# Attention with two head mixes and two MLPs on one core: the second mix on eight 64x32 tiles with VectorE transposes, and PSUM as four shared pairs of banks

## The chip, the cores and the metric

One core of a Trainium2 chip. The metric is device time in microseconds for one execution of the whole program (median of three runs); the profile is of one further execution of the same kernel. TensorE is PE in the rows (PEld its weight loads), VectorE DVE, ScalarE ACT, GpSimd POOL, SyncE SP.

## The reference

Four batches, 12 heads, 448 positions, 64 wide. The scores of all heads are mixed across heads before the softmax and the weights are mixed across heads after it; then two MLPs (768 to 2048 to 768) run over 1792 tokens.

```python
scores = scale * np.matmul(q, k.transpose(0, 1, 3, 2))
scores = np.einsum('bhij,hg->bgij', scores, w_pre)        # first mix
attn = exp(scores - max) / (sum + 1e-09)
attn = np.einsum('bhij,hg->bgij', attn, w_post)           # second mix
x = np.matmul(attn, v)                                    # tokens x 768
h = x @ moe_w_in;   x = (s * relu(h) ** 2 + b) @ moe_w_out
h = x @ moe2_w_in;  out = (h * cos(h)) @ moe2_w_out
```

## The kernel before

A planner (`Plan`) holds every step with a position, an engine (or a choice of ACT and DVE), a cost, what it comes after and which places of which ring it takes. `Plan.run` walks through time and gives each engine that is free the ready step with the lowest position; the instructions are then written in that order, so each engine's queue is fixed when the kernel is built. `STEP`, `OFF`, `W1`, `AVP` and the like are the numbers that set positions.

The attention works on blocks of 120 or 110 query rows. For each pair of heads, `heads` transposes k and q on TensorE (L306), four pieces of 112 x 128 each, and copies them out of PSUM. `scores` (L336) multiplies q by k for the two heads of a pair on the two 64-row halves of the array; each result (110 or 120 rows x 448) is copied to `s` and goes by DMA into `m`, where the 12 heads x 5 query rows (60) lie on the partitions, and two such groups make a tile of 10 query rows. There are 180 tiles, done in 90 pairs. For each pair of tiles:

- `mix` (L393): four matmuls, 60x64 weights `wp`, 448 columns, on four 64x64 tiles of the array, into two banks `p`.
- `rmax` (L403): a maximum of each bank on DVE, twice. `expo` (L409): the exponential of each bank on ACT, with a sum, twice.
- DVE adds 1e-9 (L412) and takes the reciprocal (L413); `weigh` (L417, POOL) multiplies the mix matrix by it into `w`.
- `mixt` (L427): the second mix. The exponentials `e` are the weights, 60 x 112 keys at a time, and `w` (60 columns) is what moves: 16 matmuls, on the two 64-row halves, which puts the keys on the partitions of the result `a` (112 x 480, one bank for each tile).
- `keep` (L235 on DVE or L233 on ACT): each bank is copied into `at`, which holds a half batch.

When a half batch is complete, `prod` (L464) multiplies it by v for four heads at a time: 16 matmuls of 230 or 220 columns over 112 keys, on two 64-column tiles, and `xo` is copied and stored to `x`. There are 24 such products. PSUM's eight banks are split: two for scores, transposes and products with v (ring `ps`), two for the second mix (`pa`), four for the first mix (`pp`).

The MLPs (L704, L767, L797) begin when their token columns of `x` are loaded, and their weights are prepared on ACT, DVE and POOL (L626 to L654). Every fp32 matmul of the attention stands in the trace as two LDWEIGHTS and two MATMUL records.

Of the kernel before, what the change touches and what calls it, by code (L numbers as in the profile page):

```python
# [10 lines left out]
F32 = mybir.dt.float32  # L11
# [5 lines left out]
ALU = mybir.AluOpType  # L17
# [5 lines left out]
CH = 112  # L23
TOKENS = (512, 512, 256, 512)
# [6 lines left out]
class Hold:  # L31


    def __init__(self, ring):
        self.ring, self.users, self.tile = ring, 0, None


class Plan:
# [5 lines left out]
    def __init__(self):  # L44
        self.steps, self.cap, self.turns = [], {}, {}
# [7 lines left out]
    def hold(self, ring):  # L53
        return Hold(ring)
# [14 lines left out]
    def run(self):  # L69
# [30 lines left out]
        def blocked_until(i, t):  # L100
# [3 lines left out]
            for h in st[i]["take"]:  # L104
                k = need.get(h.ring, 0)
# [11 lines left out]
        while n_done < len(st):  # L117
# [7 lines left out]
            while again:  # L125
                again = False
                for e in free:
# [34 lines left out]
                    for h in s["take"]:  # L162
                        taken[h.ring].append(h)
                    for h in s["use"]:
                        h.users -= 1
                        if not h.users:
                            freed_at[h] = end + s["lag"] + self.SYNC[e]
                            heapq.heappush(events, freed_at[h])
# [26 lines left out]
STEP = 2374.9  # L195
# [3 lines left out]
def attention(pl, tc, q, k, v, w_pre, w_post, cst, x, mid, left, right, psl, psr):  # L199
# [6 lines left out]
    NG = H // 2  # L206

# [42 lines left out]
    def idle(pos, n, cost, after):  # L250
        hz = pl.hold("ps")

        def run():
            hz.tile = ps_s.tile([128, 512], F32, tag="s", name="idle")
# [7 lines left out]
    mask = one.tile([128, 2, G], F32, name="mask")  # L262
    w12 = one.tile([128, 2, H], F32, name="w12")
    wp = one.tile([128, 64], F32, name="wp")
    wq = one.tile([128, H, G], F32, name="wq")
    d_id = dma(-5200, lambda: ident, lambda: cst[:, 0:128], 65536, cost=450.0)
    d_mk = dma(-500, lambda: mask.rearrange("p a g -> p (a g)"), lambda: cst[:, 128:128 + 2 * G], 5120)
    z0 = pl.add(-9e9, "dve", 100.0, lambda: (nc.vector.memset(w12, 0.0), nc.vector.memset(wp, 0.0)))
# [7 lines left out]
        out=wq, in0=w12[:, 1].rearrange("p (g o) -> p g o", o=1).to_broadcast([128, H, G]),  # L276
        in1=mask[:, 0].rearrange("p (o r) -> p o r", o=1).to_broadcast([128, H, G]), op=ALU.mult), d_w + [d_mk])
# [6 lines left out]
    at_all = at_p.tile([128, 2, 4, H, width[0]], F32, name="at")  # L284
# [3 lines left out]
    def heads(what, b, g, p):  # L288
        src = k if what == "k" else q
        ht = turned[what, b, g] = pl.hold(f"{what}{g}")  # L290
        hr, hp = scratch[what == "q"] if b == 0 else pl.hold("r"), pl.hold("ps")

        def raw(new=False):
            if b == 0:
                i = g * 8 * D
                return at_all[:CH, int(what == "q")].rearrange("p c h w -> p (c h w)")[:, i:i + 8 * D].rearrange("p (z h d) -> p z h d", h=2, z=4)
            if new:
                hr.tile = r_p.tile([CH, 4, 2, D], F32, tag="r", name="raw")
            return hr.tile
        d = dma(p - 6000, lambda: raw(True), lambda: src[b, 2 * g:2 * g + 2].rearrange("h (p z) d -> p z h d", z=4), CH * 8 * D * 4,  # L300
                [s_open] if b == 0 else [], take=[hr] if b else [], behind=m_done[0][-1:] if b else [], two=b == 0 and g < 2, rate=300.0)

        def trans():
            hp.tile = ps_s.tile([128, 512], F32, tag="s", name="t" + what)[:, :S].rearrange("p (z w) -> p z w", z=4)
            for z in range(4):
                nc.tensor.transpose(hp.tile[:, z], raw()[:, z].rearrange("p h d -> p (h d)"), ident[:CH, :CH])  # L306
        a = pl.add(p, "pe", 400.0, trans, [d, d_id], take=[hp, ht], use=[hr])

        def evac(e):
# [45 lines left out]
    for g in range(NG):  # L355
        for what in "kq":
            heads(what, 0, g, PRO[0] * g)
# [521 lines left out]
```

## Time and profile before

| | us |
|---|---|
| median of 3 runs (1410.46 to 1412.24) | 1411.2 |
| profiled execution, its own time | 1410.2 |
| its span in the trace | 1408.4 |
| PE busy | 1383.4 (98%) |
| DVE busy | 1095.8 (78%) |
| ACT busy | 665.8 (47%) |
| POOL busy | 429.7 (31%) |
| mean granted TensorE clock | 0.982 |

How to read it: the first second mix starts at 51 us and the last products with v end at 474 us; from about 498 us on PE runs MLP matmuls without a break. Matmuls overlap, and the ends of their records are modelled, so that the busy share of PE says little; the chain of waits, which gives each stretch of time to one cause, says more.

### The profile page before, as it was taken

The numbers are of one execution on the slowest core, as the hardware profiler recorded it, in microseconds if no ns is written. First come the engines' busy times: TensorE is split into PE (matmuls) and PEld (weight loads), VectorE is DVE, ScalarE is ACT, GpSimd is POOL, SyncE is SP. The second block draws the span as 40 slices with busy tenths as digits, with TensorE's granted clock in tenths as the row PEclk, the third lists the DMA queues.
The fourth block names the chain that finished last, engine by engine and source line by source line (L and its number), as shares of the span: only waits on it lengthen the run. The fifth ranks groups of instructions, "written<-read, shape, count | busy, mean of one in ns | idle before, by whom it ended". The sixth has DMA issues, their size and how long they took to land.

```text
span 1408.4 us, 25444 instructions
## 1 busy us (share of the span) xinstructions
PE 1383.4 (98%) x9753; PEld 1103.6 (78%) x9753; DVE 1095.8 (78%) x2052; ACT 665.8 (47%) x1385; POOL 429.7 (31%) x415
## 2 busy tenths in 40 slices
PE   7999999999999899999999999999999999999999
PEld 3466565666666688888888888889999999899998
DVE  3566666576577688889887787898799999998975
ACT  1575465465467454323232232466645545445442
POOL 2010000010012443423333243235554444554531
PEclk6899999999999999999999999999999999999999
DMA  6645456444444422221121212112121111211103
GB/s 132 183 129 146 143 138 156 138 130 140 139 148 141 142 68 68 68 67 58 54 71 34 67 47 65 36 34 68 46 68 46 57 57 45 69 45 57 56 35 123
DMA packets 120605, 123.80 MB, mean 88 GB/s; under 512 B 49476, under 2 KB 108324, under 8 KB 120484
## 3 DMA queue, kind: packets, MB, share of 16 engines
q1 hardware_dynamic: 117880, 120.43, 29.6%
q10 hardware_dynamic: 2604, 1.75, 0.5%
q8 instruction: 77, 1.26, 0.4%
q14 instruction: 44, 0.36, 0.1%
HBM read 72.43 MB, written 11.01 MB: 59 GB/s over the span
## 4 chain that ended last, share of the span: by engine, by line
PE 96%; DVE 1%; DMA 1%; ACT 1%; SPq 0%; issue 0%; POOL 0%; DVEq 0%; POOLq 0%
PE h L704 33%; PE o L797 17%; PE o L767 16%; PE a L427 11%; PE sps L336 7%; PE p L393 6%; PE vps L464 5%; PE tq L306 1%; PE tk L306 1%; DMA m<-s 0%; SPq L229 0%; DMA at<-in_q_dram 0%; DMA m<-x 0%; DVE s L235 0%; DVE x L680 0%
## 5 line engine op out<-in xcount | busy, mean ns | idle before, releaser
L652 POOL TENSOR_TENSOR cm<-ca,wh 128x384 f32<-128x384 f32 x128 | 160.8, 1258 | 363.3 <-ACT wh L646 362.6
L704 PE MATMUL h<-m,wh 128*128 128x512 f32 x672 | 217.0, 392 | 0.0
L704 PE MATMUL h<-x,wh 128*128 128x512 f32 (+1 forms) x768 | 192.0, 341 | 5.2 <-DVE x L680 3.8
L427 PEld LDWEIGHTS a<-w,e 60*112 60x112 f32 x2880 | 153.6, 176 | 50.8 <-issue 29.3
L654 POOL TENSOR_TENSOR wl<-cm,ce 128x384 fp32r<-128x384 f32 x128 | 147.5, 1154 | 93.4 <-DVE ce L650 87.3
L427 PE MATMUL a<-w,e 60*112 60x60 f32 x2880 | 161.6, 261 | 3.7 <-POOL w L417 3.5
L417 POOL TENSOR_TENSOR w<-wq,st 128x120 f32<-128x120 f32 x90 | 35.5, 396 | 396.5 <-DVE st L413 306.9
L704 PEld LDWEIGHTS h<-x,wh 128*128 128x128 f32 x768 | 133.0, 190 | 22.5 <-DVE x L680 4.8
L704 PE MATMUL h<-m,wl 128*128 128x512 f32 x384 | 150.6, 392 | 0.0
L704 PEld LDWEIGHTS h<-m,wh 128*128 128x128 f32 x672 | 125.4, 188 | 25.8 <-issue 0.7
L767 PE MATMUL o<-gl,wh 128*128 128x512 f32 (+1 forms) x384 | 139.6, 364 | 0.0
L767 PE MATMUL o<-gh,wl 128*128 128x512 f32 (+1 forms) x384 | 139.6, 364 | 0.0
L409 ACT ACTIVATE e<-p,st 128x448 f32<-128x448 f32 x180 | 113.2, 630 | 55.4 <-DVE st L403 41.6
L767 PE MATMUL o<-gh,wh 128*128 128x512 f32 (+1 forms) x384 | 139.3, 363 | 0.0
L704 PE MATMUL h<-x,wl 128*128 128x512 f32 (+1 forms) x384 | 130.9, 341 | 0.0
L403 DVE TENSOR_REDUCE st<-p 128x1 f32<-128x448 f32 x180 | 109.5, 618 | 21.7 <-PE p L393 19.4
L336 PE MATMUL sps<-kt,qt 64*110 64x448 f32 (+1 forms) x384 | 109.3, 613 | 6.7 <-DVE s L235 5.3
L797 PE MATMUL o<-wh,gl 128*128 128x384 f32 x448 | 114.3, 335 | 0.0
L797 PE MATMUL o<-wh,gh 128*128 128x384 f32 x448 | 114.2, 335 | 0.0
L797 PE MATMUL o<-wl,gh 128*128 128x384 f32 x448 | 114.2, 335 | 0.0
L744 POOL TENSOR_TENSOR tb<-ta,tb 128x512 f32<-128x512 f32 (+1 forms) x64 | 79.0, 1234 | 114.3 <-ACT tb L742 109.4
L806 DVE TENSOR_TENSOR acc<-acc,o 128x384 f32<-128x384 f32 x196 | 99.7, 545 | 14.3 <-PE o L797 14.2
(86 smaller groups left out, 2616.6 us busy)
## 6 DMA issues: line engine op xcount, KB each, us to landing
m<-s SPq DMA_DIRECT2D x144, 192.5 KB
raw<-in_moe_w_in_dram SPq DMA_DIRECT2D x64, 384.0 KB
raw<-in_moe_w_out_dram SPq DMA_DIRECT2D x64, 384.0 KB
m<-s SPq DMA_DIRECT2D x42, 210.0 KB
v<-in_v_dram SPq DMA_DIRECT2D x12, 448.0 KB
out_dram<-acc SPq DMA_DIRECT2D x13, 384.0 KB
raw<-in_k_dram SPq DMA_DIRECT2D x18, 224.0 KB
raw<-in_q_dram SPq DMA_DIRECT2D x18, 224.0 KB
```

The lines of the kernel that those rows point to most:

```text
L336: nc.tensor.matmul(out=hp[z].tile, lhsT=hq.tile[64 * z:64 * z + 64, i0:i0 + rows], rhs=hk.tile[64 * z:64 * z + 64], start=True, stop=True, ...
L393: nc.tensor.matmul(out=hp[y].tile[64 * z:64 * z + 64], lhsT=wp[64 * y:64 * y + (K if y else 64)], rhs=src[64 * y:64 * y + (K if y else 64) ...
L403: nc.vector.tensor_reduce(out=hst.tile[:, 0, y:y + 1], in_=hp[y].tile, axis=AX, op=ALU.max, negate=True)
L409: nc.scalar.activation(out=he.tile[:, y], in_=hp[y].tile, func=AF.Exp, bias=hst.tile[:, 0, y:y + 1], accum_out=hst.tile[:, 1, y:y + 1])
L427: nc.tensor.matmul(out=ha[z].tile.rearrange("p (c g r) -> p c g r", c=4, g=H)[:, c, :, y * G:(y + 1) * G], lhsT=he.tile[64 * z:64 * z + K, ...
L652: a = pl.add(p0 + 6 * dp, "pool", 1050, lambda hm=hm, ha=ha, flat=flat: nc.gpsimd.tensor_tensor(out=hm.tile, in0=ha.tile.bitcast(F32), in1 ...
L654: got.append(pl.add(p0 + 7 * dp, "pool", 1050, lambda hm=hm, he=he, flat=flat: nc.gpsimd.tensor_tensor(out=flat(1), in0=hm.tile, in1=he.ti ...
L704: nc.tensor.matmul(out=hp.tile, lhsT=w, rhs=cols(z_, j, k)[:, 0], start=(k == 0 and y == 0), stop=(k == KD - 1 and y == 2))
L744: a = pl.add(p + 7 * dp, "pool", n * 2.4 + 100, lambda h1=h1, h2=h2: nc.gpsimd.tensor_tensor(out=h2.tile, in0=h1.tile, in1=h2.tile, op=ALU ...
L767: nc.tensor.matmul(out=hp.tile, lhsT=w, rhs=x, start=(c == 0 and y == 0), stop=(c == 1 and y == 2))
L797: nc.tensor.matmul(out=hp[e].tile, lhsT=x, rhs=w[:, e * HD:(e + 1) * HD], start=(c == 0 and y == 0), stop=(c == 1 and y == 2))
L806: got.append(pl.add(p, "dve", 470, lambda e=e, hp=hp, view=view: nc.vector.tensor_tensor(out=view(), in0=view(), in1=hp[e].tile, op=ALU.ad ...
```

## The change

The second mix is turned round: `w` is now the weights, in pieces of 32 columns (6 heads x 5 rows and two columns of zeros), and `e` moves, 224 columns at a time. The 16 matmuls of a pair go to eight tiles of 64 rows x 32 columns. The result has the mixed rows on the partitions, so `keep` is now a VectorE transpose of 32x32 blocks, one for both banks of a pair (94 in all, 86 of them of two banks), and `at` has the keys on 64-partition halves, one half for each six heads. The product with v has 28 matmuls over 64 keys on four 64x64 tiles, in place of 16 over 112 keys on two; what moves there are pieces of 5 elements, 32 apart. v is loaded by two DMAs per four heads in place of one, in rows of 256 bytes.

PSUM is four tiles of two banks each (`bank`), and scores, transposes (now k and q together), both mixes and the products with v all take one such pair, whichever comes free first; at most two each for the first mix, the second mix, and the rest. One `tensor_reduce` takes the maximum of both banks. The addition of 1e-9 goes from DVE to POOL. k is now written with the same order of columns as q.

```diff
@@ Plan
+    def places(self, name, n):
+
+        self.slots[name] = [0.0] * n
...
+                if h.ring in self.slots:
+                    open_at = [a for z, a in enumerate(self.slots[h.ring]) if a is not None and (h.only is None or z in h.only)]
+                    if not open_at:
+                        return None
+                    when = max(when, min(open_at))
+                    continue
@@ attention
-    ps_s = pool(psl, "a_ps_s", N_PS, space=PSUM)
-    ps_a = pool(psl, "a_ps_a", N_PA, space=PSUM)
-    ps_p = pool(psr, "a_ps_p", N_PP, space=PSUM, side="right")
+    ps_l = pool(psl, "a_ps_l", space=PSUM)
+    ps_r = pool(psr, "a_ps_r", space=PSUM, side="right")
+    bank = [(ps_r if z > 1 else ps_l).tile([128, 2, 512], F32, name=f"ps{z}") for z in range(4)]
+    pl.places("u", 4)
...
-    at_all = at_p.tile([128, 2, 4, H, width[0]], F32, name="at")
+    NU = width[0] // G
+    at_all = at_p.tile([128, 2, KB, NU * 32], F32, name="at")
...
-        a = pl.add(p, "pe", 400.0, trans, [d, d_id], take=[hp, ht], use=[hr])
+        a = pl.add(p, "pe", 860.0, trans, [load["k"], load["q"], d_id], take=[hp, lim, ht["k"], ht["q"]], use=[hr["k"], hr["q"]])
...
-            copy(e, ht.tile.rearrange("p (w z) -> p z w", z=4) if what == "q" else ht.tile.rearrange("p (z w) -> p z w", z=4), hp.tile)
+                copy(e, ht[what].tile.rearrange("p (w z) -> p w z", z=4), bank[hp.slot][:, y, :S].rearrange("p (z w) -> p w z", z=4))
...
+        for z in range(2):
+            got.append(dma(p, lambda z=z: v_all[64 * z:64 * z + 64, c], lambda z=z: v[b, GH * z + 2 * c:GH * z + 2 * c + 2].rearrange("h (k p) d -> p (h k) d", p=64),
+                           64 * 2 * KB * D * 4, take=[] if z else [hv], behind=got[:1] + m_done[0][-1:], rate=200.0))
...
-        hp, hs = [pl.hold("ps"), pl.hold("ps")], pl.hold("s")
+        hp, lim, hs = pl.hold("u"), pl.hold("ps"), pl.hold("s")
...
-        hp, ha = [pl.hold("pp"), pl.hold("pp")], [pl.hold("pa"), pl.hold("pa")]
+        last = i >= NTL // 2 - 2
+        hp, ha = pl.hold("u", (2, 3) if last else None), pl.hold("u", (0, 1) if last else None)
+        limp, lima = pl.hold("pp"), pl.hold("pa")
...
-                nc.vector.tensor_reduce(out=hst.tile[:, 0, y:y + 1], in_=hp[y].tile, axis=AX, op=ALU.max, negate=True)
+            nc.vector.tensor_reduce(out=hst.tile[:, 0], in_=hp.tile, axis=AX, op=ALU.max, negate=True)
...
-        a = pl.add(p - OFF[3] * STEP, "dve", 75, lambda hst=hst: nc.vector.tensor_scalar(out=hst.tile[:, 2], in0=hst.tile[:, 1], scalar1=1e-9, scalar2=None, op0=ALU.add), got)
+        a = pl.add(p - OFF[3] * STEP, "pool", 200, lambda hst=hst: nc.gpsimd.tensor_tensor(out=hst.tile[:, 2], in0=hst.tile[:, 1], in1=eps, op=ALU.add), got)
...
-            for c in range(4):
-                for y in range(2):
-                    for z in range(2):
-                        nc.tensor.matmul(out=ha[z].tile.rearrange("p (c g r) -> p c g r", c=4, g=H)[:, c, :, y * G:(y + 1) * G], lhsT=he.tile[64 * z:64 * z + K, y, c * CH:(c + 1) * CH],
-                                         rhs=hw2.tile[64 * z:64 * z + K, y], start=True, stop=True, tile_position=(64 * z, 0))
+            for y in range(2):
+                for u in range(2):
+                    for c in range(2):
+                        for z in range(2):
+                            o = 64 * u + 32 * c
+                            nc.tensor.matmul(out=ha.tile[o:o + 32, z].rearrange("p (y k w) -> p y k w", y=2, w=32)[:, y], lhsT=hw2.tile[64 * z:64 * z + K, y, 32 * u:32 * u + 32],
+                                             rhs=he.tile[64 * z:64 * z + K, y].rearrange("p (k c w) -> p k c w", c=2, w=32)[:, :, c], start=True, stop=True, tile_position=(64 * z, o))
...
-                copy(e, at_all[:CH, slot].rearrange("p c h w -> p (c h) w")[:, :, col:col + R], h.tile.rearrange("p (c r) -> p c r", r=R))
+                nc.vector.transpose(out=at_all[:, slot].rearrange("p k (u w) -> p u k w", w=32)[:, unit:unit + 2 * m].rearrange("p (z y) k w -> p z y k w", y=2),
+                                    in_=h.tile[:, z:z + m].rearrange("p z (y k w) -> p z y k w", y=2, w=32))
...
+                for k in range(KB):
+                    for y in range(2):
+                        for z in range(2):
+                            w = (2 * pp + y) * G
+                            nc.tensor.matmul(out=bank[hp.slot][64 * y:64 * y + 64, z, :n].rearrange("p (u r) -> p u r", r=G), lhsT=v_all[64 * z:64 * z + 64, pp, y * KB + k],
+                                             rhs=at_all[64 * z:64 * z + 64, hf, k, :n // G * 32].rearrange("p (u w) -> p u w", w=32)[:, :, w:w + G],
+                                             start=(k == 0), stop=(k == KB - 1), tile_position=(64 * z, 64 * y))
...
-STEP = 2374.9
+STEP = 3468.7
...
-OFF = (2.256, 2.164, 1.349, -0.066)
+OFF = (2.847, 0.745, -0.81, 1.669)
```

The planner's costs and position numbers change too, so that the order of the steps is another one on every engine. The change names L393 as L426, L427 as L459, L464 as L498, L336 as L369, and its PSUM tiles ps_96 to ps_99 (one pair of banks each).

PE's queue where the products with v of the first batch's second half run, before (p is the first mix, a the second, sps the scores, vps a product with v):

```order
L336 MATMUL sps<-kt,qt 110x448 x2
L393 MATMUL p<-m,wp 64x448 x8
L427 MATMUL a<-w_1528,e 112x12x5 x16
L336 MATMUL sps<-kt,qt 110x448 x2
L427 MATMUL a<-w_1541,e 112x12x5 x16
L464 MATMUL vps<-at,v 64x220 x16
L427 MATMUL a<-w_1625,e 112x12x5 x16
L464 MATMUL vps<-at,v 64x220 x16
L393 MATMUL p<-m,wp 64x448 x4
```

The same stretch in the change:

```order
L426 MATMUL ps_98<-m,wp 64x448 x4
L459 MATMUL ps_96<-e,w_1306 32x224 x16
L369 MATMUL ps_99<-kt,qt 110x448 x2
L426 MATMUL ps_97<-m,wp 64x448 x4
L369 MATMUL ps_96<-kt,qt 110x448 x2
L459 MATMUL ps_99<-e,w_1348 32x224 x16
L369 MATMUL ps_98<-kt,qt 110x448 x2
L426 MATMUL ps_96<-m,wp 64x448 x4
L498 MATMUL ps_99<-at,v 64x220 x28
L459 MATMUL ps_97<-e,w_1380 32x224 x16
```

A second mix still has 16 matmuls, now 32 rows x 224 columns each; a product with v has 28 in place of 16; and all kinds of step take turns on the same four pairs ps_96 to ps_99.

VectorE's queue in the attention, before (st is a maximum, a sum or its reciprocal, at the kept second mix):

```order
L235 COPY at<-a 112x48x10
L235 COPY s<-sps 110x448
L403 TENSOR_REDUCE st<-p 128x1
L235 COPY at<-a 112x48x10
L403 TENSOR_REDUCE st<-p 128x1
L235 COPY s<-sps 110x448
L403 TENSOR_REDUCE st<-p 128x1
L412 TENSOR_SCALAR st<-st 128x2
L413 RECIPROCAL st<-st 128x2
```

And in the change:

```order
L473 STREAM_TRANSPOSE at<-ps_96 128x4x7x32
L433 TENSOR_REDUCE st<-ps_97 128x2
L433 TENSOR_REDUCE st<-ps_98 128x2
L473 STREAM_TRANSPOSE at<-ps_99 128x4x7x32
L258 COPY s<-ps_96 110x448
L444 RECIPROCAL st<-st 128x2
L258 COPY s<-ps_96 110x448
L433 TENSOR_REDUCE st<-ps_97 128x2
L444 RECIPROCAL st<-st 128x2
```

Each maximum and each transpose covers two banks, half of the kept second mixes no longer go to ACT, and the additions are gone from this queue. In VectorE's whole queue of the change stand 90 maxima, 94 transposes, 90 reciprocals, 80 copies of scores (102 before), 21 of k and q (24 before) and 48 of xo of half the length (34 whole ones before).

## Rows read from the trace of the kernel before

**Rows 1.** Busy time by stretch: stretch, its length, PE, PEld, DVE, ACT, POOL (counts), granted clock, DMA share, GB/s
```profile
0.00:50.00 50.00, 39.69 (x122) 15.15 (x123) 16.92 (x30) 10.19 (x20) 9.26 (x5) 0.62 0.70 157
50.00:440.00 390.00, 386.68 (x4565) 247.01 (x4563) 259.23 (x578) 228.03 (x547) 35.48 (x88) 1.00 0.50 143
440.00:500.00 60.00, 52.06 (x399) 40.66 (x400) 41.84 (x82) 30.64 (x67) 23.24 (x19) 0.89 0.39 123
500.00:1408.00 908.00, 905.02 (x4673) 800.76 (x4671) 777.84 (x1364) 396.97 (x755) 361.75 (x304) 1.00 0.19 58
```

**Rows 2.** The chain of waits from 50 to 440 us, shares by engine and line
```profile
by line: PE a L427 36.7%; PE p L393 20.0%; PE sps L336 19.1%; PE vps L464 17.3%; PE tq L306 2.1%; PE tk L306 1.8%; DVE qt L235 0.5%; DVE at L235 0.5%; DVE st L403 0.5%; issue 0.4%; ACT xo L233 0.3%; ACT qt L233 0.3%; POOL w L417 0.2%; ACT e
```

**Rows 3.** The same chain, pieces in order of time: start us, us, what
```profile
200.53 0.80 PE sps L336 x4
201.33 0.91 PE p L393 x8
202.24 1.71 PE a L427 x32
203.96 3.26 PE vps L464 x32
207.21 0.53 PE tk L306 x4
207.75 1.72 PE a L427 x32
```

**Rows 4.** Second mix by groups, 50 to 440 us: count | busy us, mean ns | idle before
```profile
L427 PE MATMUL a<-w,e 60*112 60x60 f32 x2720 | 151.2, 259 | 0.9 <-POOL w L417 0.7
L427 PEld LDWEIGHTS a<-w,e 60*112 60x112 f32 x2720 | 143.9, 175 | 45.6 <-issue 27.9 <-POOL w L417 15.3 <-POOL cm L652 0.7
```

**Rows 5.** VectorE by groups, 50 to 440 us
```profile
L403 DVE TENSOR_REDUCE st<-p 128x1 f32<-128x448 f32 x171 | 104.1, 618 | 17.4 <-PE p L393 15.2 <-POOL w L417 0.6
L235 DVE COPY s<-sps 110x448 f32<-110x448 f32 (+1 forms) x93 | 57.4, 622 | 8.2 <-PE sps L336 4.9 <-ACT e L409 0.2
L235 DVE COPY at<-a 112x480 f32<-112x480 f32 x86 | 56.4, 658 | 58.8 <-PE a L427 58.5
L235 DVE COPY xo<-vps 128x220 f32<-128x220 f32 (+1 forms) x32 | 17.8, 556 | 26.9 <-PE vps L464 26.3
L412 DVE TENSOR_SCALAR st<-st 128x2 f32<-128x2 f32 x85 | 14.1, 166 | 12.4 <-ACT e L409 12.2
L413 DVE RECIPROCAL st<-st 128x2 f32<-128x2 f32 x85 | 13.8, 162 | 2.0
```

**Rows 6.** ScalarE by groups, 50 to 440 us
```profile
L409 ACT ACTIVATE e<-p,st 128x448 f32<-128x448 f32 x172 | 108.2, 630 | 52.8 <-DVE st L403 39.0 <-DVE st L412 11.8 <-DVE st L413 1.6
L233 ACT ACTIVATE at<-a 112x480 f32<-112x480 f32 x84 | 48.5, 579 | 66.9 <-PE a L427 66.7
L233 ACT ACTIVATE qt<-tq 128x448 f32<-128x448 f32 x16 | 15.7, 982 | 20.2 <-PE tq L306 20.2
L233 ACT ACTIVATE kt<-tk 128x448 f32<-128x448 f32 x6 | 3.3, 543 | 2.1 <-PE tk L306 2.1
```

**Rows 7.** Busy time in a stretch of the MLPs, columns as in rows 1
```profile
560.00:700.00 140.00, 140.00 (x706) 118.82 (x705) 123.54 (x207) 43.51 (x82) 48.86 (x42) 1.00 0.21 62
```

**Rows 8.** Who waited for whom, 50 to 440 us: us in total, times, longest
```profile
POOL w L417 <- DVE st L413: 298.1, 61, 40.2
```

**Rows 9.** PE in order of time, start of the program: start us, us, what [idle before]
```profile
28.74 1.85 PE L336 MATMUL sps<-kt,qt 64*120 64x448 f32 x4 [0.77 <-DVE s L235]
31.34 1.85 PE L336 MATMUL sps<-kt,qt 64*120 64x448 f32 x4 [0.75 <-DVE s L235]
44.24 3.27 PE L393 MATMUL p<-m,wp 64*64 64x448 f32 x16
```

**Rows 10.** PE in order of time, end of the attention
```profile
451.44 3.24 PE L427 MATMUL a<-w,e 60*112 60x60 f32 x32 [2.21 <-POOL w L417]
487.24 0.51 PE L704 MATMUL h<-x,wh 128*128 128x512 f32 x1 [2.75 <-DVE x L680]
```

More of the change, by code (lines that the diff above doesn't have):

```diff
@@ L44, in __init__ @@
     def __init__(self):
[L45 removed]
+        self.steps, self.cap, self.turns, self.slots = [], {}, {}, {}
     def ring(self, name, cap, strict=True):
@@ L162, in run @@
                     for h in s["take"]:
-                        taken[h.ring].append(h)
+                        if h.ring in self.slots:
+                            w = self.slots[h.ring]
+                            h.slot = min((a, z) for z, a in enumerate(w) if a is not None and (h.only is None or z in h.only))[1]
+                            w[h.slot] = None
+                        else:
+                            taken[h.ring].append(h)
                     for h in s["use"]:
@@ L352, in scores @@
             m_done[n].append(dma(p + 1300, lambda z=z: place(z), lambda z=z: hs.tile[:rows, z], rows * S * 4, ev[z:z + 1], take=[hm] if g == 0 and z == 0 else [], use=[hs],
-                                 behind=m_done[n][:1], cost=870.0, two=n == 0))
+                                 behind=m_done[n][:1], cost=770.0, two=n == 0))
     for g in range(NG):
-        for what in "kq":
-            heads(what, 0, g, PRO[0] * g)
+        heads(0, g, PRO[0] * g)
         scores(0, g, PRO[0] * g + PRO[1])
@@ L429, in attention @@
-        a = pl.add(p, "pe", MIXT, mixt, [aw], take=ha, use=[he, hw2])
-        for z, t in enumerate(pair):
-            n, b_ = t["n"], t["b"]
-            half = (b_, (n % 4) // 2)
+            ha.tile = bank[ha.slot][:, :, :2 * KB * 32]
+            for y in range(2):
[5 more added lines that the diff above has]
+                                             rhs=he.tile[64 * z:64 * z + K, y].rearrange("p (k c w) -> p k c w", c=2, w=32)[:, :, c], start=True, stop=True, tile_position=(64 * z, o))
@@ L433, in attention @@
+        a = pl.add(p, "pe", MIXT, mixt, [aw], take=[ha, lima], use=[he, hw2])
+        halves = [t["n"] // 2 for t in pair]
+        for z in (0, 1) if halves[0] != halves[1] else (0,):
+            n, m = pair[z]["n"], 1 if halves[0] != halves[1] else 2
+            half = (n // 4, (n % 4) // 2)
             new = half not in hat
@@ new lines, in attention, with evac @@
+            a = pl.add(p + apart * 2 * pp, "pe", 2880.0, prod, kept[b, hf] + v_done[b, pp], take=[hp, lim], use=[hb, vh[b, pp]])
+            got = []
+            for z in range(2):
+                def evac(e, z=z, hp=hp, ho=ho, blocks=blocks, base=base, wid=wid):
+                    if z == 0:
+                        ho.tile = xo_p.tile([128, 2 * width[0]], F32, tag="xo", name="xo")[:, :2 * wid].rearrange("p (g n) -> p g n", g=2)
+                    c0 = 0
+                    for i0, rows in blocks:
+                        copy(e, ho.tile[:, z, i0 - base:i0 - base + rows].rearrange("p (r t) -> p r t", r=R), bank[hp.slot][:, z, c0:c0 + rows].rearrange("p (t r) -> p r t", r=R))
+                        c0 += rows
+                got.append(pl.add(p + apart * (2 * pp + 1) + 500, EV, (420.0, 420.0), evac, [a], take=[] if z else [ho], use=[hp, lim], behind=got[:1]))
+                if not late:
+                    free_psr.append(got[-1])
```

187 lines of the change are left out of this document (91 added, 96 removed).

## The prediction

> **What bounds the kernel now.** I read the busy time by stretch first, then the chain of waits, then the groups of each engine. The stretches divide the program [rows 1]: a start of 50 us at a granted clock of 0.62, the attention from 50 to 440 us at full clock, a passage of 60 us in which PE is idle for 8 us, and 908 us of MLPs in which PE is idle for 3. The change touches nothing in the last of these, so its effect must come out of the first three, above all out of 390 us of attention. There PE is idle for only 3.3 us [rows 1], but a busy PE is not PE at its peak; what matters is what each step takes on the chain. The chain of that stretch is 97% PE [rows 2]: second mix 36.7%, first mix 20.0%, scores 19.1%, products with v 17.3%, transposes 3.9%. VectorE is busy for 259 of the 390 us (66%) and ScalarE for 228 (58%) [rows 1]. So PE sets the pace here, and a shorter step on PE is worth its length as long as the other engines follow.
>
> **What a step on PE costs.** A first mix is 8 records of 448 columns on four tiles, so 2 rounds or 896 columns if the four work at once: 0.91 us [rows 3]. A product with v is 32 records of 230 columns on two tiles, 16 rounds or 3,680 columns: 3.26 us [rows 3]. The difference is 2.35 us for 2,784 columns, 0.844 ns a column, and what is left of a step is 0.154 us. Two and four tiles thus go with the same price, which says that tiles do work at once. By the same price a second mix, 32 records of 60 columns on two tiles, would take 16 x 60 x 0.844 ns + 0.154 = 0.96 us. It takes 36.7% of 390 us over 85 mixes (2,720 records of 32 each [rows 4]) = 1.68 us [rows 2]. Something other than columns that move holds it: (1.68 - 0.154) / 32 = 47.8 ns for each pair of a weight load and a matmul. Each load brings 112 columns of weights; in first mix and products it brings 64 and hides. 112 columns in 47.8 ns is 2.3 a ns, which at the granted full clock (2.4 GHz) is about one a cycle. I read it as the loads being in the way, one after the other.
>
> **The change, part by part.**
>
> *Second mix.* 32 records again, but of 32 columns of weights and 224 that move, on eight tiles: 4 rounds or 896 columns, 0.91 us, if all eight work at once and the loads (32 columns, about 14 ns at the rate above) hide. No row shows eight tiles or a load of 32 columns. From below: 0.91. From above: 48 ns for each pair whatever its width, or four tiles at once (8 rounds, 1.67 us), which both leave the 1.68 as it is; two at once would be worse and is a rival below. I take 0.91, since two and four tiles follow the price by columns: 90 x (1.68 - 0.91) = **-69.3 us**. The Trainium skill (TensorE: Matmul & The Clock Gate, "Wait — 56ns, not 53.3ns?") says that two matmuls never start closer than about 25 ns, however small. By it a mix would be 32 x 25 ns + 0.154 = 0.95 us, and the gain 4 us smaller; no row here has matmuls that close.
>
> *Product with v.* 56 records on four tiles: 14 rounds in place of 16. 14 x 230 x 0.844 ns + 0.154 = 2.87 us against 3.26, and 2.75 against 3.12 for 220 columns: 24 x 0.38 = **-9 us**. What moves are pieces of 5, which no row shows on PE; if that doubled the price of a column, it would cost 24 x 2.7 = +65 us. I take no charge and keep it as a rival.
>
> *Transposes of k and q together.* 24 steps in place of 48: 24 x 0.154 is 3.7, and half of it is hidden behind a neighbour of the same kind already: **-2 us** (0 to -4). Copies of k and q lie between the two that rows 6 shows, 0.54 and 0.98 us; either way it is a few us off the path.
>
> *VectorE.* One maximum over two banks: a row of 480 elements against one of 448 [rows 5] gives (658 - 622) / 32 = 1.1 ns an element, so 0.618 + 448 x 1.1 ns = 1.11 us against 2 x 0.618. The transpose of two banks has no row; by elements it is the same 1.11, against 0.658 for one bank on VectorE and 0.579 for the other on ScalarE [rows 5, 6]. In the stretch: maxima 94, transposes 94, reciprocals 14, scores 57.4 x 80/102 = 45, k and q some 14, xo 16, additions 0: 277 us in place of 259. ScalarE loses 48 us of copies [rows 6]. PE's own path shrinks to 390 - 85 x 0.77 - 21 x 0.38 - 2 = 314 us. VectorE would have to be busy for 88% of that. It is at 88% in a stretch of the MLPs where PE never waits [rows 7], so it can be; but in the attention each step crosses three engines several times, and now all kinds of step draw on the same four pairs of banks. A first mix holds a pair for about 0.9 + 1.1 + 2 x 0.83 us and the gaps between, over 4 us; a second mix over 2, scores about 2, a product with v about 4. Per pair of tiles that is some 10 us of pairs against 4 x 3.5 that there are, 70%. So PE will wait at times where it waits hardly at all now. Bounds: nothing (88%, rows 7), or VectorE at its present 66%, which would need 420 us and undo the gain. I take 83%, nearer to rows 7, where PE is also the one that sets the pace: 334 us, **+20 us** of new waits on PE.
>
> *Addition on POOL.* One more hop between the sums and the weights of the second mix. POOL is busy for 35 of 390 us [rows 1] and spends 298 us waiting for the reciprocal [rows 8]; nothing stands behind it but the next addition. The mixes run ahead of PE by more than a hop, so it costs nothing except where the queue is empty, at the end, where PE waits 2.21 us for the weights [rows 10]: at most 0.3 us a mix for the last three.
>
> *DMA.* 12 more issues on SP for v, and smaller rows; the transfers' share is 0.50 in the attention [rows 1] and would be about 0.6 with the same bytes in less time. Hidden; a late v would first be seen before a product with v.
>
> *Start.* The score steps wait about 0.75 us each, seven times, for a copy out of their only two banks [rows 9]; with four pairs two steps can be open. But the first mix, at 44.24 us, also waits for the transfers into `m`: **-2 us** (0 to -5). *Passage to the MLPs*: 8 us idle [rows 1], with 2.75 for the split of x [rows 10]; the same loads and copies follow the last product with v: 0 (-6 to +6).
>
> Sum: -69.3 - 9 - 2 + 20 - 2 = -62. The profiled execution took 1410.2 us for its span of 1408.4, and the median is 1.0 above it: 1410.2 - 62 + 1 = **1349 us**.
>
> **The rivals.**
>
> 1. *VectorE sets the pace.* If it gets no further than 75%, its 277 us need 369, a gain of 21 in the stretch and 7 outside it: **1383 us**; at 71% nothing is left of the stretch's gain. For it: maxima and transposes are long, and a pair of banks stays closed behind each. Against: rows 7. The Trainium skill (TensorEngine Tiling (Array Packing), "PSUM Bottleneck") speaks for it: tiling makes TensorE faster but not the way out of PSUM, which can become the bound. The rows so far agree that this is where the margin is, 66% going to over 80%. Chance 0.15.
> 2. *The second mix keeps its 1.7 us*, because 48 ns is the price of a pair of load and matmul, or because four tiles is all that work at once. Then 9 + 4 us are left: **1398 us**. The 48 ns fits both readings; the nearness to one column a cycle speaks for mine. Chance 0.08.
> 3. *The pieces of 5 slow the product with v.* At double the price of a column the 65 us eat the gain, less some of the 20 us of waits: about **1408 us**. The Trainium skill (SBUF — State Buffer, "Door 1: The DMA port swizzle", its note on lines) says that reads which leave a 16-byte line cost extra; each piece of 20 bytes spans two lines. No row shows what that costs PE. Chance 0.03.
> 4. *Slower: the four column tiles of a row half take turns*, so that only two of the eight, one in each half, work at once. A second mix is then 16 x 224 x 0.844 ns + 0.154 = 3.18 us, 90 x 1.50 = +135 us, less 13: **1533 us**. It decides at 1.82 us a mix, that is under 3.6 tiles at once. Against it: first mixes run four at once now, with two column tiles in each row half. Chance 0.08.
>
> **How the numbers follow.** My forecast has 0.66, with a range of its own from 1325 (no new waits, a quicker start) to 1380. Rivals 1 to 4 have 0.15, 0.08, 0.03 and 0.08. From 1325 to 1400 lie the forecast, rival 1 and most of rival 2, some 0.85. A measurement of this kernel can tell about 0.2%, 3 us, from no change. Faster: 0.66 + 0.15 + 0.06 = 0.87. Same: 0.02 of rival 2 and 0.02 of rival 3. Slower: rival 4 and 0.01 of rival 3, 0.09.
>
> **What would show it.** In the chain of the attention a second mix of 0.9 us, as long as a first mix; a product with v of 2.87; the transpose of two banks at 1.1; VectorE above 80% and PE with some 20 us of waits for VectorE or ScalarE. The attention would end some 60 us earlier, and the MLPs take as long as now. I am wrong if a second mix stays above 1.2 us, if a transpose takes 1.5 or more, or if PE waits for over 40 us.

## The result, and the profile after

The change took **1329.0 us** (median of 4 runs, 1327.71 to 1329.58) where the kernel before took 1410.8 (4 runs, 1408.8 to 1412.24): a ratio of 0.942 [0.9403, 0.9436]. That is 82 us less where 62 were forecast; the direction and the range held, and 20 us are to be explained. The profiled execution took 1328.4 us for a span of 1326.6.

Three points of the program cut the 82 us into parts. The first record of a second mix on PE starts at 39.34 us (51.13 before): **-11.8**. From there to the end of the last second mix, where the next MLP matmul starts, it is 341.3 us (407.9 before): **-66.6**. From there to the first matmul of the MLPs' output it is 30.3 us (39.0 before), and the rest takes 915.6 (910.4 before): **-3.5** together, since 12 matmuls of the hidden layer moved from the one side of that point to the other.

Busy time by stretch of the change, columns as in [rows 1]:

```profile
0.00:50.00 50.00, 35.12 (x253) 15.36 (x257) 19.50 (x35) 17.77 (x40) 11.32 (x13) 0.90 0.92 173
50.00:370.00 320.00, 309.00 (x4976) 147.59 (x4972) 242.98 (x393) 180.51 (x497) 50.76 (x167) 0.99 0.65 171
370.00:400.00 30.00, 24.97 (x347) 17.59 (x348) 28.52 (x49) 14.97 (x38) 11.16 (x16) 0.94 0.51 149
420.00:1327.00 907.00, 901.84 (x4655) 797.49 (x4653) 779.38 (x1364) 396.98 (x754) 364.58 (x304) 1.00 0.19 58
```

The MLPs are as they were (PE 902 of 907 us against 905 of 908). The attention is 70 us shorter, VectorE is busy for 243 of 320 us, 76% where it was 66%, and the DMA share is 0.65 where it was 0.50.

The chain of waits of the change from 40 to 380 us, shares by engine and line, which answers to [rows 2]:

```profile
by line: PE ps L369 18.4%; PE ps L459 18.1%; PE ps L426 16.3%; PE ps L498 14.4%; DMA raw<-in_q_dram 6.7%; DMA m<-s 6.3%; PE ps L336 4.0%; ACT e L440 2.8%; issue 2.6%; DVE st L433 1.7%; DMA raw<-in_moe_w_in_dram 1.5%; ACT s L256 1.4%; SPq L2
```

And pieces of it in order of time (start us, us, what), which answer to [rows 3]:

```profile
180.72 0.91 PE ps L426 x8
181.63 0.92 PE ps L459 x32
182.55 1.71 PE ps L369 x8
...
187.25 2.96 PE ps L498 x56
190.21 0.94 PE ps L369 x4
191.15 0.92 PE ps L459 x32
192.07 1.01 PE ps L336 x8
```

A second mix (L459) is as long as a first mix (L426): 0.92 us where it was 1.7. A product with v (L498) is 2.96 us here and 2.8 to 3.0 elsewhere. PE's share of the chain has fallen from 97% to 71%: transfers of q and of `m` now stand in it with 13%. That does not mean that PE waited for 13% of the time. By these durations the work of PE from 50 to 370 us is 84 first mixes x 0.91, 83 second mixes x 0.92, 82 score steps x 0.85, 21 products x 2.9 and 18 pairs of transposes x 1.0, some 302 us of 320. By this estimate some 18 us are left for waits (the chain before left 3% of 390, 12 us), and the records show PE idle for 11 (3.3 before). The chain shows through which work the end was reached, and there are now several ways that are nearly as long.

Groups of instructions from 50 to 370 us, for VectorE, ScalarE and PE, columns as in [rows 4]:

```profile
L433 DVE TENSOR_REDUCE st<-ps 128x2 f32<-128x896 f32 x83 | 88.9, 1073 | 8.0 <-PE ps L426 7.9
L473 DVE STREAM_TRANSPOSE at<-ps 128x896 f32<-128x896 f32 x79 | 87.2, 1108 | 12.3 <-PE ps L459 8.8 <-ACT xo L256 1.2 <-ACT s L256 1.2
L459 PE MATMUL ps<-e,w 60*32 60x224 f32 x2656 | 81.8, 357 | 0.8 <-ACT s L256 0.5
...
L256 ACT ACTIVATE kt<-ps 128x448 f32<-128x448 f32 x12 | 6.5, 544 | 9.2 <-PE ps L336 9.1
L258 DVE COPY qt<-ps 128x448 f32<-128x448 f32 x9 | 5.6, 624 | 5.4 <-ACT kt L256 5.4
L256 ACT ACTIVATE qt<-ps 128x448 f32<-128x448 f32 x9 | 4.9, 542 | 4.4 <-DVE kt L258 4.4
```

The transpose of two banks is 1.108 us and the maximum of two banks 1.073. A copy of k or of q now takes 0.54 us on ScalarE; a copy of q took 0.98 before [rows 6].

PE in order of time at the start of the change (start us, us, what [idle before]), which answers to [rows 9]:

```profile
16.89 1.81 PE L369 MATMUL ps<-kt,qt 64*120 64x448 f32 x4 [0.83 <-ACT qt L256]
25.71 4.02 PE L369 MATMUL ps<-kt,qt 64*120 64x448 f32 x20 [1.36 <-ACT qt L256]
33.66 2.95 PE L426 MATMUL ps<-m,wp 64*64 64x448 f32 x16 [3.93 <-DMA v<-in_v_dram]
39.34 0.99 PE L459 MATMUL ps<-e,w 60*32 60x224 f32 x32 [0.44 <-ACT e L440]
```

From 25.71 us on, 20 records of scores run in 4.02 us with no wait between, 0.80 us for four. Before, four took 1.85 us, with 0.75 of waiting ahead of each [rows 9]. The granted clock tells why they differ in length too. The kernel before by stretch:

```profile
15.00:25.00 10.00, 9.25 (x23) 3.92 (x22) 3.18 (x7) 2.05 (x3) 0.00 (x0) 0.50 0.36 89
25.00:35.00 10.00, 7.09 (x18) 2.03 (x16) 2.50 (x4) 2.17 (x4) 0.00 (x0) 0.50 0.43 134
35.00:45.00 10.00, 6.99 (x18) 1.65 (x18) 1.87 (x3) 2.17 (x4) 0.00 (x0) 0.50 0.86 212
```

And the change:

```profile
15.00:25.00 10.00, 7.04 (x24) 3.07 (x24) 3.84 (x8) 3.25 (x6) 0.00 (x0) 0.66 0.66 157
25.00:35.00 10.00, 5.36 (x32) 2.45 (x36) 2.58 (x5) 2.72 (x5) 0.00 (x0) 0.95 0.88 181
35.00:45.00 10.00, 8.16 (x105) 2.56 (x100) 6.37 (x10) 5.44 (x15) 1.79 (x6) 0.88 0.88 183
```

Before, PE stood at 1.2 GHz from 15 to 45 us and did every score step at half speed; in the change it is at 2.4 GHz for nearly all of 25 to 35 us, and then waits 3.93 us for transfers ahead of the first mix.

### The profile page after: what moved, and what is told of

The parts are those of the page before. It is cut to its first block, busy times and chain, and to the rows that moved or that the text cites. A ratio compares the mean times of both kernels' runs of the same rounds, so it can differ in the third digit from the quotient of the medians.

```text
span 1326.6 us, 26575 instructions
## 1 busy us (share of the span) xinstructions
PE 1290.8 (97%) x10329; PEld 994.9 (75%) x10329; DVE 1086.2 (82%) x1868; ACT 622.8 (47%) x1353; POOL 449.3 (34%) x505
## 4 chain that ended last, share of the span: by engine, by line
PE 87%; DMA 5%; DVE 3%; SPq 2%; ACT 1%; issue 1%; POOL 0%; DVEq 0%; ACTq 0%; POOLq 0%
PE h L743 33%; PE o L836 18%; PE o L806 17%; PE ps L369 5%; PE ps L459 5%; PE ps L498 4%; PE ps L426 4%; DMA raw<-in_q_dram 2%; DMA m<-s 2%; SPq L252 1%; PE ps L336 1%; ACT e L440 1%; DVE st L433 1%; ACT s L256 0%; PE ps L743 0%
## 5 line engine op out<-in xcount | busy, mean ns | idle before, releaser
L743 PE MATMUL h<-m,wh 128*128 128x512 f32 x648 | 208.1, 390 | 0.0
L743 PE MATMUL h<-x,wh 128*128 128x256 f32 (+1 forms) x768 | 189.5, 338 | 0.0
L743 PE MATMUL h<-m,wl 128*128 128x512 f32 x372 | 145.6, 391 | 0.0
L743 PEld LDWEIGHTS h<-m,wh 128*128 128x128 f32 x648 | 120.8, 188 | 24.0
L440 ACT ACTIVATE e<-ps,st 128x448 f32<-128x448 f32 x180 | 112.8, 634 | 54.6 <-DVE st L433 42.8
L473 DVE STREAM_TRANSPOSE at<-ps 128x896 f32<-128x896 f32 (+1 forms) x94 | 99.7, 1067 | 14.9 <-PE ps L459 11.2
L813 DVE TENSOR_TENSOR acc<-acc,o 128x512 f32<-128x512 f32 (+1 forms) x168 | 101.0, 614 | 7.6 <-PE o L806 7.0
L685 ACT ACTIVATE wh<-ca 128x384 fp32r<-128x384 f32 x128 | 65.8, 519 | 87.8 <-DVE ca L674 68.7
L369 PE MATMUL ps<-kt,qt 64*110 64x448 f32 (+1 forms) x384 | 96.2, 597 | 9.5 <-ACT qt L256 3.6
L433 DVE TENSOR_REDUCE st<-ps 128x2 f32<-128x896 f32 x90 | 96.3, 1074 | 10.5 <-PE ps L426 10.5
```

The source lines that it names most:

```text
L369: nc.tensor.matmul(out=bank[hp.slot][:rows, z, :S], lhsT=hq.tile[64 * z:64 * z + 64, i0:i0 + rows], rhs=hk.tile[64 * z:64 * z + 64], start ...
L433: nc.vector.tensor_reduce(out=hst.tile[:, 0], in_=hp.tile, axis=AX, op=ALU.max, negate=True)
L440: nc.scalar.activation(out=he.tile[:, y], in_=hp.tile[:, y], func=AF.Exp, bias=hst.tile[:, 0, y:y + 1], accum_out=hst.tile[:, 1, y:y + 1])
L473: nc.vector.transpose(out=at_all[:, slot].rearrange("p k (u w) -> p u k w", w=32)[:, unit:unit + 2 * m].rearrange("p (z y) k w -> p z y k ...
L743: nc.tensor.matmul(out=hp.tile, lhsT=w, rhs=cols(z_, j, k)[:, 0], start=(k == 0 and y == 0), stop=(k == KD - 1 and y == 2))
L813: a = pl.add(p, "dve", n * 1.05 + 66, lambda hp=hp, view=view: nc.vector.tensor_tensor(out=view(), in0=view(), in1=hp.tile, op=ALU.add), [ ...
```

## The experiments

My theory after the result: the second mix is short because weight loads are paid by their columns, and 32 columns hide where 112 did not; and PE can use that only because every step may take any of the four pairs of banks. The rivals: one half of the change alone does most of it; VectorE is already the bound; the missing 20 us were transfers.

### The two halves apart

First the sharing alone, with the old second mix, copies and product (its core, against the change). Here, and in the next one, keys stand in another order in k than in v, which changes what comes out and none of the work.

```diff
-            ha.tile = bank[ha.slot][:, :, :2 * KB * 32]
+            ha.tile = bank[ha.slot][:CH, :, :4 * R * H]
...
-                nc.vector.transpose(out=at_all[:, slot]...
+                copy(e, at_all[:CH, slot]..., h.tile[:, z].rearrange("p (c r) -> p c r", r=R))
```

> The second mix (exponentials as weights of 112 columns), its copies by VectorE or ScalarE and the product with v over 112 keys as before the change; the four shared pairs of banks, the joint maximum and the addition on POOL as in the change; the order is planned anew. Theory (the gain is TensorE's time in these two steps, and the rest comes from the start and from the banks): second mix 1.68 us and product 3.26 in the chain again, 69 + 9 us more than the change less some 10 us of waits that go under longer steps, so about 1397 us; the first mix still starts near 34 us as in the change. Rival (the shared banks pay for most of the gain, and the tiles for little): below 1365 us.

Measured 1397.9 us, ratio 0.9929 [0.9867, 0.9991]: some 12 us, with an interval from 1 to 19, and the first second mix comes at 41.26 us, early as in the change. The stretch of the second mixes itself is not shorter than before (417 us from the first record of one to the last, against 408).

Then the new second mix, transposes and product alone, with PSUM divided 2, 2, 4 as before (its core, against the kernel before):

```diff
-                h.tile = ps_a.tile([128, 512], F32, tag="a", name="a")[:CH, :4 * R * H]
+                h.tile = ps_a.tile([128, 512], F32, tag="a", name="a")[:, :2 * KB * 32]
...
-                copy(e, at_all[:CH, slot]...
+                nc.vector.transpose(out=at_all[:, slot]..., in_=h.tile.rearrange("p (y k w) -> p y k w", y=2, w=32))
```

> The second mix on eight 64x32 tiles, VectorE transposes (one for each bank) and the product with v over 64 keys as in the change; PSUM's banks divided 2, 2, 4, two maxima and the addition on VectorE as before; the order is planned anew. Theory: second mix 0.91 and product 2.87 us, 78 us less than before less new waits of 10 to 20 us, and a start like before (first mix near 44 us): about 1345 us, 16 more than the change. Rival (without shared pairs PE can't use the shorter mix, since scores and products have only two banks): PE waits over 40 us, 1375 us or more.

Measured 1377.2 us, ratio 0.9765 [0.9705, 0.9825]: 33 us, where PE's prices alone give the 78 that the prediction adds up for mix and product. The second mix is 0.92 us here too, but PE is busy for 327.90 of the 350 us from 50 to 400. Waits in that stretch (engine, line, what it waited for: us in total, times, longest):

```profile
PEld sps L342 <- ACT s L235: 20.2, 33, 1.4
...
PE p L399 <- DMA m<-s: 6.1, 4, 3.5
```

The weight loads of the score steps wait for ScalarE to copy the scores out of their two banks. PE, which has earlier work to run meanwhile, is idle for 28.8 us between its first and its last second mix (19.1 in the change, 6.1 before), and the largest single cause is the transfers into `m`. That stretch is 31 us longer than in the change, so the waits for the banks are not shown to be all of it. 12 and 33 us apart, 82 together: the shorter step paid in full only together with the shared banks and the joint steps (one maximum for two banks, one transpose of two banks, k and q transposed together). The start of this kernel is that of before, 0.50 of the clock from 15 to 45 us, and its first second mix comes at 49.90 us, so it is the half with the pairs and the joint transposes that quickens the start.

### The free choice of a pair

The change with its four pairs reserved: one for scores, transposes and products, one for the second mix, two for the first; and then two, one, one.

```diff
-        hp, lim = pl.hold("u"), pl.hold("ps")
+        hp, lim = pl.hold("u", (0,)), pl.hold("ps")
...
-        hp, ha = pl.hold("u", (2, 3) if last else None), pl.hold("u", (0, 1) if last else None)
+        hp, ha = pl.hold("u", (2, 3)), pl.hold("u", (1,))
```

> The change with its four pairs reserved as the banks were before: one pair for scores, transposes and products with v, one for the second mix, two for the first mix; everything else as in the change (joint maximum, addition on POOL, copies of k); the order is planned anew. Theory (the free choice of a pair is what lets PE use the shorter mix: the one pair of scores, transposes and products is held for about 2.2 + 0.6 + 1.0 = 3.8 us per pair of tiles, 342 us in all, as long as PE's own work): 1365 us or more, like the run with the new mix in the old division. Rival (that run was slow for its two maxima, its own transposes per bank or its order): under 1345.

```diff
-        hp, lim = pl.hold("u"), pl.hold("ps")
+        hp, lim = pl.hold("u", (0, 1)), pl.hold("ps")
...
-        hp, ha = pl.hold("u", (2, 3) if last else None), pl.hold("u", (0, 1) if last else None)
+        hp, ha = pl.hold("u", (3,)), pl.hold("u", (2,))
```

> The change with its four pairs reserved 2, 1, 1: two pairs for scores, transposes and products, one for the second mix, one for the first mix; the order is planned anew. Theory (a first mix holds its pair for about 0.9 + 1.1 + 2 x 0.83 us and gaps, 4.2 us, 378 us in all with a single pair): slower than with the division 1, 1, 2, 1375 us or more. Rival (only scores and products lack room): faster than that division, 1345 or less.

Measured 1401.4 us (ratio to before 0.9931 [0.9911, 0.9952]) and 1410.7 (1.001 [0.9989, 1.0031]): 72 and 82 us above the change. Waits from 50 to 400 us of the first:

```profile
PEld ps L369 <- DVE s L258: 22.6, 21, 2.4
PEld ps L369 <- ACT s L256: 21.3, 19, 3.5
```

And of the second:

```profile
PEld ps L426 <- ACT e L440: 69.5, 50, 2.2
...
PE ps L426 <- ACT e L440: 39.4, 34, 1.8
```

With one pair for the scores, PE's loads wait for the copies of scores; with one pair for the first mix, PE and its loads wait for the exponentials that hold it. The wait moves to whatever has one pair. The start shows the same. Busy time of its 50 us with one pair for the scores, columns as in [rows 1]:

```profile
0.00:50.00 50.00, 29.41 (x93) 13.24 (x93) 9.56 (x21) 8.90 (x15) 9.26 (x5) 0.58 0.59 123
```

And with two:

```profile
0.00:50.00 50.00, 31.70 (x207) 13.62 (x209) 17.70 (x33) 15.41 (x32) 11.04 (x11) 0.93 0.87 170
```

With one pair, which is what the kernel before had for them, the granted clock is 0.58 (0.62 before) and the first second mix comes at 56.95 us; with two it is 0.93 (0.90 in the change) and 38.97 us (39.34). So 17.6 of the first run's 72 us lie in the start, and none of the second's 82. A caution holds for the four runs so far, the late v and whatever else below changes a ring: the planner writes another order for each, with position numbers that were set for another kernel, so part of the 72 us may be order and not division. How large that part can be shows in the new mix with the old division above: it took 1377.2 us, 24 less than the change with the same reservation, though it lacks the joint steps as well.

One pair taken away from all of them:

```diff
-    pl.places("u", 4)
+    pl.places("u", 3)
```

> The change with three shared pairs of banks in place of four (the fourth stays unused); the order is planned anew. Theory (pairs are used for about 70%, so with three they would be used for over 90%): PE waits 30 us or more, 1360 us or above, with the waits of PE's loads on ACT and DVE copies. Rival (pairs have room, the new waits come from transfers): under 1340.

Measured 1369.5 us in one run, 40 above the change. In these runs three pairs that anyone may take are better than four with reservations.

### What holds the second mix

The kernel before with half of the weight columns (56 of 112, so half of the keys), its order kept:

```diff
-... lhsT=he.tile[64 * z:64 * z + K, y, c * CH:(c + 1) * CH],
+... lhsT=he.tile[64 * z:64 * z + K, y, c * CH:c * CH + CH // 2],
```

> The kernel before with weights of 56 columns in place of 112 in the second mix: it leaves out every second group of 56 keys in the second mix and in the product with v; same number of instructions, same moving columns. Theory (loads go one after the other, by their columns): a second mix drops from 1.68 us to the price of its moving columns, 0.96, and the time by some 60 us to about 1350. Rival (48 ns for each pair of a load and a matmul, whatever the width): second mix still 1.68 us, time 1410.

Measured 1356.1 us in one run. Second mixes in its chain of waits (start us, us, what):

```profile
156.00 0.83 PE a L427 x32
164.24 1.02 PE a L427 x32
176.57 0.98 PE a L427 x32
186.53 0.98 PE a L427 x32
```

With as many matmuls, moving as much, a second mix falls from 1.7 us to 0.83 to 1.02. So neither the number of pairs nor what moves set its time; the columns of weights did. What holds it at 56 columns can't be told: half of 47.8 ns for each of 32 pairs and 0.154 us are 0.92, and the moving columns alone were 0.96 in the prediction.

How the loads follow each other is another question. The prediction read the 47.8 ns as loads "one after the other". Records of the second mix before that are open in 10 ns (stretch, its length, PE, PEld, clock, DMA):

```profile
202.35:202.36 0.01, 0.01 (x4) 0.01 (x2) 1.00 0.16 26
202.36:202.37 0.01, 0.01 (x4) 0.01 (x4) 1.00 0.00 0
...
202.45:202.46 0.01, 0.01 (x6) 0.01 (x2) 1.00 0.00 0
202.46:202.47 0.01, 0.01 (x6) 0.01 (x4) 1.00 0.00 0
```

Two loads begin within the same 10 ns at 202.36, two more at 202.46, and none between. By the order in the program the two are those of the two 64-row halves. A pair of loads every 98 ns is the same price for the step as one load every 47.8, but it speaks for two loads side by side, each at half the rate. Every kernel here uses both halves, so no run parts the two readings.

Then the change with every matmul of the second mix cut in two (128 and 96 columns), which doubles the pairs and leaves the columns that move as they are:

```diff
-                for u in range(2):
-                    for c in range(2):
+                for k0, k1 in ((0, 4), (4, KB)):
+                    for u, c in ((0, 0), (0, 1), (1, 0), (1, 1)):
...
-... rhs=he.tile[64 * z:64 * z + K, y].rearrange("p (k c w) -> p k c w", c=2, w=32)[:, :, c], ...
+... rhs=he.tile[64 * z:64 * z + K, y].rearrange("p (k c w) -> p k c w", c=2, w=32)[:, k0:k1, c], ...
```

> The change with each matmul of the second mix split in two, of 128 and 96 moving columns: 64 records in place of 32, the same 896 columns per tile, same order otherwise. Theory (price by columns, eight tiles at once): 0.91 us a mix and 1329 us, at most 4 us more. Rival by a floor of about 25 ns between two matmuls: 64 x 25 ns + 0.15 = 1.75 us a mix, 75 us more less waits that go under it, about 1395. Rival by 48 ns for each pair: 3.2 us a mix, over 1500.

Measured 1344.1 us in one run. Second mixes in its chain of waits (64 records each, of which some are missing in the trace):

```profile
140.31 1.03 PE ps L459 x59
149.10 1.03 PE ps L459 x59
152.74 1.03 PE ps L459 x59
```

64 pairs in 1.03 us are (1.03 - 0.154) / 64 = 13.7 ns for a pair, and 32 columns at the 47.8 ns per 112 of the prediction are 13.7 ns. That fits a split step that is again held by its loads, at the same price per column; a lowest price of a pair whatever its width would fit this one width as well. The time that I expected (no more than 4 us above the change) was too low because of it. The Trainium skill (TensorE: Matmul & The Clock Gate, "Wait — 56ns, not 53.3ns?") puts a floor of about 25 ns between the starts of two matmuls. The change alone could not tell, as its 32 pairs take 24 ns each; here 64 matmuls start within 1.03 us, one every 16 ns, so the floor does not hold for matmuls on eight tiles. The prediction found no matmuls that close in its rows; the trace of before has them, four matmuls of a first mix that start 6 to 7 ns apart.

### How near VectorE is

Each transpose done twice, the order kept:

```diff
                 nc.vector.transpose(out=at_all[:, slot]..., in_=h.tile[:, z:z + m]...)
+                nc.vector.transpose(out=at_all[:, slot]..., in_=h.tile[:, z:z + m]...)
```

> The change with every VectorE transpose done twice into the same place: 94 more instructions of about 1.07 us, 99.7 us of VectorE; same order otherwise. VectorE is busy for 243 of the 320 us from 50 to 370 us in the change (76%). Theory (VectorE has a margin but not a large one): 243 + 92 us need 381 us at 88% busy, so the time rises by 40 to 65 us, to 1370 to 1394. Rival (VectorE is far from the path, PE and the transfers set the pace): under 1345.

Measured 1398.9 us in one run, 70 more, for 94 transposes of 1.1 us or some 100 us. Busy time of a stretch, columns as in [rows 1]:

```profile
50.00:420.00 370.00, 306.10 (x4748) 139.63 (x4748) 315.77 (x455) 171.90 (x474) 46.52 (x159) 0.98 0.55 145
```

And one of the waits in it:

```profile
PEld ps L369 <- DVE at L475: 27.8, 21, 2.9
```

VectorE is at 85%, PE at 83%, and the two transposes take 13.6% and 10.0% of the chain. Of some 100 us of added work about 30 found room beside PE and 70 did not. So the change, at 76%, is not held by VectorE throughout, but there is little left. The second transpose (L475) also holds its pair of banks for 1.1 us more, and loads of score steps wait for that, so this run does not part VectorE's time from the time of the banks. The Trainium skill (TensorEngine Tiling (Array Packing), "PSUM Bottleneck") warns of just this way out of PSUM; the run agrees that the margin there is small, with 70 us lost of 100 added, and in the change PE is still idle for only 11 of 320 us.

### The transfers

The chain named transfers of q and of `m`. The loads of v for the first batch held back until the transfers into `m` of the third block of query rows are through, so that they don't stand beside them:

```diff
-... behind=got[:1] + m_done[0][-1:], rate=200.0))
+... behind=got[:1] + m_done[0][-1:] + m_done[2][-1:], rate=200.0))
```

> The change with the six loads of v of the first batch held back until the last transfer of the third block's scores has been issued. Theory (at the start the small rows of v sit between the transfers into m that the first mixes wait for; PE waits 3.9, 1.7 and 3.4 us there): 4 to 8 us less, about 1323. Rival (the transfers into m are late by themselves): 1329 within 2.

Measured **1325.4 us** (1323.25 to 1326.22), ratio to before 0.9388 [0.9372, 0.9405]: 3.6 us under the change (1327.71 to 1329.58) and the best of all. It is a small step, 0.3%, but the two sets of four runs do not overlap. Busy time of two stretches, in the change:

```profile
45.00:55.00 10.00, 5.06 (x88) 1.81 (x80) 5.43 (x9) 4.79 (x14) 1.39 (x5) 0.98 0.84 178
55.00:65.00 10.00, 9.91 (x96) 3.13 (x100) 6.40 (x11) 2.98 (x7) 0.60 (x2) 0.68 0.52 163
```

And here:

```profile
45.00:55.00 10.00, 9.66 (x137) 3.29 (x129) 8.08 (x14) 5.88 (x16) 2.09 (x7) 1.00 0.45 143
55.00:65.00 10.00, 8.85 (x164) 3.37 (x148) 9.71 (x15) 5.94 (x17) 1.45 (x6) 1.00 0.71 194
```

In the change PE is busy for half of 45 to 55 us, and the clock granted next is 0.68; with the loads of v out of the way PE works through, and the clock stays. Its first mix itself comes later (35.80 us against 33.66), so the gain is smaller than the waits that went.

Then a fourth buffer for the raw k and q, of which a joint transpose holds two; alone, and with the late v:

```diff
-    r_p = pool(right, "a_r", 3, side="right")
+    r_p = pool(right, "a_r", 4, side="right")
...
-... ("m", 2), ("r", 3),
+... ("m", 2), ("r", 4),
```

> The change with four buffers for raw k and q in place of three. Theory (a step now takes k and q together, so of three buffers one at most is free to load ahead, and PE waits for q at each change of batch, 8.9 us in all in PE's own queues and 6.7% of the attention's chain): 4 to 10 us less, about 1322. Rival (other waits take their place): 1329 within 2.

> The change with the loads of v of the first batch held back and four raw buffers, both as in the two runs before. Theory (four raw buffers were slower only because the late v did not come with them and the order fell badly): 1320 to 1330. Rival (a load that starts sooner takes from the transfers into m): 1340 or more.

Measured 1345.8 us (0.9531 [0.9509, 0.9552]) and 1344.5 (0.9528 [0.9511, 0.9545]): 17 and 19 us **slower** than the same without it, against what I expected of both. From 40 to 400 us PE and its loads wait for raw k and q for 5.9 us in the first run, 3.0 of it for raw k, where they waited 8.9 in the change, all of it for raw q: a third of these waits went. The planner writes another order too, and PE is less busy in some stretches: from 300 to 350 us for 45.03 us in the first and 49.83 in the change, from 150 to 200 for 46.24 and 49.45. So these runs do not show what the waits for raw k and q cost in an order like that of the change, and why this order is worse stays open.

## Why the prediction came out as it did

- **Second mix, -69.3: right.** 0.92 us against 0.91, at the lower of the two ends, and for the reason given, that the columns of weights held it: with half of them the old step fell to 0.83 to 1.02 us, and twice the pairs with 32 columns took the 13.7 ns each that the price per column says. That the loads go "one after the other" is not shown; the records of before start two at a time. Rivals 2 and 4 (1.7 us, 3.18 us) fall with it.
- **Product with v, -9: right.** 2.8 to 3.0 us in the chain against 2.75 and 2.87. The pieces of 5 cost no more than some 0.1 us a product in these rows, so rival 3 falls. The note on lines (the Trainium skill, SBUF — State Buffer, "Door 1: The DMA port swizzle") does not show in PE's time here.
- **VectorE's steps: right.** 1.108 us for the transpose against 1.11, 1.073 for the maximum against 1.11.
- **New waits, +20: too many, it was some +13.** From the first second mix to the end of the last the time fell by 66.6 us, where the steps -69.3 - 9 - 2 with the +20 make -60; most of these steps lie in it, so the waits are some +12 to +14 by difference. The records give the same: PE is idle there for 19.1 us in the change and 6.1 before. I had taken 83% for VectorE, 277 us of work in 334; it is at 76%, 243 in 320. The 277 adds up groups, whose times overlap, and was set beside the 259 for which VectorE was busy: the six groups of [rows 5] alone add up to 263.6. Counted alike, as a sum of all records, it is 280 us before and 263 in the change, so VectorE's work fell where the prediction had it grow by 18. This is 7 of the 20 us. Rival 1, with the same 277, put VectorE's limit at 75%; doubling the transposes took it to 85%, and there the time does rise.
- **Start, -2: the step that failed.** It was -11.8, outside its own bounds of 0 to -5. The prediction priced the score steps by the 0.75 us that each waited [rows 9] and left out that each took 1.85 us there and 0.80 in the attention [rows 3], at the granted clock of 0.62 that [rows 1] shows for the start. With the waits between them mostly gone, the steps from 25.71 us on ran at 2.4 GHz; reserving one pair for the scores brought the low clock back (0.58), two pairs did not (0.93); and the first mix now waits for transfers instead. How much of the 11.8 us is waits and how much clock stays open: the old mix with the shared pairs gained 9.9 us there at a clock of only 0.60, 0.72 and 0.79 in the three stretches shown above. This is 10 of the 20 us.
- **DMA, hidden at a share of 0.6: nearly.** The share is 0.65. With the loads of v held back from those into `m`, 3.6 us went (and the order changed with it). "A late v would first be seen before a product with v" was the wrong place to look: an early v was seen, near 50 us.
- **Passage and MLPs, 0: -3.5**, within the 6 that I gave it.

## What to carry to other kernels

When a matmul step is longer than its moving columns explain, divide the rest by the weight columns: if it comes near the 47.8 ns for 112 columns of this case, turn the operands round so that the narrow one is loaded. Before counting the gain of a shorter step, ask what frees its PSUM banks; here the step and the sharing of banks gave 33 and 12 us apart and 82 together. Where a stretch shows a clock under 1, price the removal of small waits with the clock that PE would have without them. And never set a sum of groups beside a busy time: the groups' times overlap.

## What the runs showed of the hardware

- Where loads of weights bound a step on two row halves, each costs 47.8 ns for 112 columns (kernel before), and 13.7 ns for 32 with the matmuls cut in two; in the records of before the loads start two at a time, a pair every 98 ns. The matmuls of eight tiles of 64 x 32 run at once (896 columns in 0.92 us for 32 records).
- A copy out of PSUM that writes SBUF in pieces of a stride took 0.98 us on ScalarE [rows 6]; the same copy, now reading PSUM with the stride and writing SBUF in one piece, took 0.54 (542 ns above).
- A chain that names transfers for 13% of a stretch can stand beside a PE that is idle for 11 of 320 us. A fourth buffer for raw k and q, against the transfers of q that it names, took a third of PE's waits for them away and left the kernel 17 us slower, in another order.
